# Two annealed layers of linear attention and gated MLP: evacuations and feature-map halves placed engine by engine, and a buffer of its own for the turned query weights

## The chip, the cores and the metric

The kernel runs on one core of one Trainium2 chip. The metric is device microseconds of that core, the median of several executions. Matmuls run on PE (TensorE), PSUM is emptied by ACT (ScalarE) or DVE (VectorE); POOL (GpSimd) does a share of one elementwise product; SP issues DMAs.

The profile's span (first to last instruction) is about 1.8 us shorter than the timed execution, so 391.3 us of span belong to 393.2 us of time.

## The reference, cut to what matters

```python
x = A_x                                     # 2048 tokens x 512, bf16
for layer in (0, 1):                        # both layers use the same weights
    x = x + A(layernorm(x))                 # attention with a linear kernel
    x = x + B(layernorm(x))                 # MLP with a rectified gate

# A: 32 heads of 16
q, k, v = split(x @ wqkv)
pq, pk  = q @ w_phi, k @ w_phi              # per head, 16 x 16
phi(p)  = concat(softmax(p), softmax(-p))   # 32 features per head
num, den = phi(pq) @ (phi(pk)^T @ v), phi(pq) @ sum(phi(pk))
A = (num / (den + 1e-6)) @ wo
# B
B = (relu(x @ W_gate) * (x @ W_up)) @ W_down   # 1376 hidden columns
```

## The kernel before

The kernel is a list of 2,096 small operations. Each has an engine, an assumed cost, its dependencies, the buffers that it takes, and a due time out of a table of numbers that was found offline by annealing (a random step-by-step search). A list scheduler in the kernel plays the operations through on the assumed costs, always taking the one that can start first and, among those, the one with the earliest due time. The order that comes out is the order in which instructions are written. Each engine then works through its own instructions strictly in that order.

The names that the argument needs: `Wk2` and `Wq2` are key and query weights multiplied ("folded") with `w_phi`. For this they are first turned (transposed): wk by matmuls, wq by DMA transposes. `ek` and `Eq` are exponentials of keys and queries, `phiK` the key features (`ek` times reciprocal sums `sk`), `vext` the values. "erq" matmuls (`q<-R,Eq`) give numerators and denominators of the attention; they are copied from PSUM to `N` and `DS`, and a chain of small DVE steps (`m`, `w`, `pr`, `o`) makes the output `o` of it. `oT` is `o` transposed, `xnTB` the transposed normalised input of the MLP, `gu` a gate and an up block, `hT` their product.

```python
def evac(eng, due, out_, in_, deps, takes, uses, name, cols=512):
    def copy():
        (nc.scalar.copy if eng == "ACT" else nc.vector.tensor_copy)(out=out_(), in_=in_())
    return op(eng, act(cols) if eng == "ACT" else dve(cols), due, copy, deps, takes, uses, name=name)
...
# turned weights: one buffer, inside a tile that the MLP uses later
wk, wT_ = (p_h.tiles[i][:, lo:lo + NB * D].rearrange("p (b f) -> p b f", b=NB)
               for i, lo in ((0, 512), (1, 0)))
p_wT = Pool([wT_])
...
# key features: whole tiles on one engine, one tile (BOTH) split
PHI = dict(POOL=[("POOL", 32)] * 2, DVE=[("DVE", 64)], BOTH=[("DVE", 32), ("POOL", 16), ("POOL", 16)])
...
# attention of a token tile, for each of three groups of erq matmuls: N and DS always on ACT
nc.scalar.copy(out=q[:, k, 0:3] if k < 2 else q[:, :, 3], in_=ps.t[...])
...
# MLP: relu(gate) and up both evacuated by ACT, product on DVE
a = op("ACT", act(cols), due_g(f0), relu, [g_], (), [gp, gu], name="rg")
u = op("ACT", act(cols), due_g(f0), copy, [u_, a], (), [up, gu], name="ru")
a = op("DVE", dve(cols, 2), due_g(f0), times, [a, u], (), [gu, h], name="hT", port=True)
...
q_fold = fold(A_wqkv[:, 0:D], Wq2, k_fold[-1], 5000, p["QF"] - 5000, ("ACT", "DVE"), True)
...
order = arrange(ops)
with tc.manual_schedule():
    free, filling = None, True
    for o in order:
        if o.eng == "PE":
            filling = filling and o.name != "kvz"
            if filling and free is not None:     # before the first key sums: fill planned gaps
                idle(max(0, int((o.start - free - 150) / FILL)))   # with matmuls on zeros
            free = o.start + o.spent
        o.emit()
```

The softmax here doesn't subtract the row's maximum and nothing guards it: scores larger than these inputs give would overflow.

## Time and profile before

| | before |
|---|---|
| time, median | 392.84 us (392.43 to 393.45, 3 runs) |
| span of the profiled run | 391.3 us |
| busy: PE, DVE, ACT, POOL | 383.4, 272.9, 256.1, 27.6 us |
| useful matmuls, back to back | about 373.3 us |
| holes and filler between matmul starts | 13.3 us |

First the head of the page of the kernel before: span, busy time by engine, and three rows of busy tenths in 40 slices of the span.

```profile
span 391.3 us, 7634 instructions
PE 383.4 (98%) x2836; PEld 232.7 (59%) x2836; DVE 272.9 (70%) x668; ACT 256.1 (65%) x683; POOL 27.6 (7%) x32
PE   8999998999999999999999999999999999999996
DVE  6998967889999778916863477689999624223422
ACT  5999999866857626852776379997863661641631
```

PE is busy throughout, but matmuls overlap in the pipe (a 128x512 matmul lasts 379 ns in the trace, and the next one starts after 216), so short holes hide in "busy". I therefore made a ledger from the starts of the matmuls in the trace. From each start to the next I take off what the first matmul is worth back to back, columns / 2.4 + 2.7 ns. The two constants are fitted to the trace: they give 216 ns for 512 columns, of which the trace has 4 in 0.86 us, and 56 ns for 128 columns, of which it has 32 in 1.79 us. What remains is a hole. Filler matmuls on zeros are worth nothing, so their whole time counts as a hole. Summed by stage, holes (13.3), the time before the first matmul (1.26), the worth of all useful matmuls (373.3) and the time from the last matmul's start to the end (3.42) make up the span.

Next, the windows of the kernel before: for each stretch its length, then busy us and number of instructions of PE, PEld (weight loads), DVE, ACT and POOL, the granted clock, the DMA share and GB/s.

```profile
57.00:71.00 14.00, 12.09 (x110) 7.64 (x109) 10.38 (x33) 13.52 (x45) 0.02 (x1) 1.00 0.01 2
71.00:110.00 39.00, 38.71 (x397) 29.35 (x395) 35.27 (x109) 27.97 (x87) 0.00 (x0) 1.00 0.36 61
250.00:258.00 8.00, 7.22 (x70) 4.76 (x68) 7.46 (x27) 8.00 (x28) 0.00 (x0) 1.00 0.10 19
258.00:300.00 42.00, 42.00 (x419) 31.22 (x417) 39.85 (x128) 30.57 (x99) 0.00 (x0) 1.00 0.34 66
```

The two lines in which PE falls behind its stretch are the changes from queries to attention, 57 to 71 in layer 0 and 250 to 258 in layer 1. There ACT is full (13.52 of 14, 8.00 of 8). The view of waits says for whom PE waited (us in total, times, longest):

```profile
PE q L560 <- DVE zero L537: 1.3, 1, 1.3
PE q L734 <- ACT N L741: 1.1, 2, 0.7
PE b L763 <- ACT oT L567: 0.9, 2, 0.6
PE b L643 <- DMA xnTA<-xn: 0.4, 1, 0.4
```

The start, by PE's timeline (start, length, line, output <- inputs, shape, count):

```profile
1.26 3.60 PE L560 MATMUL q<-zero 128*128 128x512 bf16 x8 [1.26 <-DVE zero L537]
4.65 1.53 PE L580 MATMUL b<-ident,hT 128*128 128x128 bf16 x12
8.61 1.46 PE L560 MATMUL q<-zero 128*128 128x512 bf16 x6
11.62 0.81 PE L560 MATMUL q<-zero 128*128 128x512 bf16 x3
21.08 1.89 PE L716 MATMUL b<-xnTA,Wq 128*128 128x512 bf16 x8
```

Eight warm-up matmuls at half rate (427 ns apart), then nine fillers (6 and 3) between real work, and the first query matmul at 21.1 us.

### The profile page before, as it was taken

The page shows a single profiled execution, that of the slowest core. Times are in us where ns is not written, and L with a number is a line of the kernel's source. Part 1 is how long each engine was busy: PE and PEld are TensorE (multiplying, and loading weights), DVE is VectorE, ACT ScalarE, POOL GpSimd, SP SyncE. Part 2 cuts the span into 40 slices and gives each one's busy share as a digit, 9 for nine tenths or more (in the row PEclk, how much of TensorE's full clock was granted, in tenths as well). Part 3 has the DMA queues.
Part 4 walks back from the last instruction along what each step waited for, and adds up shares of the span by engine and source line. Part 5 has one row for each costly group of instructions (what it writes and reads, how often), then busy time and mean ns, then how long its engine had stood idle before and what let it go on. Part 6 is the DMA issues. An engine that isn't in the chain of part 4 may idle for free.

```text
span 391.3 us, 7634 instructions
## 1 busy us (share of the span) xinstructions
PE 383.4 (98%) x2836; PEld 232.7 (59%) x2836; DVE 272.9 (70%) x668; ACT 256.1 (65%) x683; POOL 27.6 (7%) x32
## 2 busy tenths in 40 slices
PE   8999998999999999999999999999999999999996
PEld 5454554867755445544577655577765544445874
DVE  6998967889999778916863477689999624223422
ACT  5999999866857626852776379997863661641631
POOL 0264550000000000000000003000000000000000
PEclk9999999999999999999999999999999999999999
DMA  7668740123443213002110010022434302001010
GB/s 230 118 165 195 179 144 1 37 42 55 94 63 56 40 40 56 13 2 41 34 36 2 4 24 0 3 41 49 87 70 82 83 0 69 13 13 62 18 44 28
DMA packets 60870, 22.83 MB, mean 58 GB/s; under 512 B 52673, under 2 KB 59809, under 8 KB 60833
## 3 DMA queue, kind: packets, MB, share of 16 engines
q1 hardware_dynamic: 60416, 21.95, 26.0%
q8 instruction: 22, 0.36, 0.4%
q10 hardware_dynamic: 416, 0.39, 0.3%
q14 instruction: 16, 0.12, 0.1%
HBM read 7.91 MB, written 2.10 MB: 26 GB/s over the span
## 4 chain that ended last, share of the span: by engine, by line
PE 85%; ACT 8%; DVE 3%; DMA 2%; issue 1%; DVEq 0%
PE b L827 35%; PE b L861 19%; PE b L763 6%; PE b L643 6%; PE b L649 5%; PE b L716 4%; PE q L679 3%; PE b L803 3%; PE q L734 3%; ACT Eq L720 2%; ACT N L741 2%; ACT ek L646 2%; DMA xnTA<-xn 1%; PE q L560 1%; DMA oT<-o 1%
## 5 line engine op out<-in xcount | busy, mean ns | idle before, releaser
L827 PE MATMUL b<-xnTB,wgu 128*128 128x128 bf16 (+2 forms) x1200 | 149.2, 279 | 0.1
L827 PEld LDWEIGHTS <-wgu 128*128 128x128 bf16 x1200 | 97.6, 98 | 43.8 <-DVE X L767 0.2
L861 PE MATMUL b<-wd,hT 128*128 128x512 bf16 (+2 forms) x363 | 83.8, 373 | 0.0
L837 DVE TENSOR_TENSOR hT<-gu 128x512 bf16<-128x512 bf16 (+1 forms) x83 | 34.0, 411 | 62.6 <-ACT gu L834 62.5
L831 ACT ACTIVATE gu<-b 128x512 bf16<-128x512 f32 (+1 forms) x83 | 49.2, 605 | 32.4 <-PE b L827 31.7
L834 ACT CAST gu<-b 128x512 bf16<-128x512 f32 (+1 forms) x83 | 48.2, 583 | 28.6 <-PE b L827 27.7
L861 PEld LDWEIGHTS <-hT 128*128 128x128 bf16 (+1 forms) x363 | 34.8, 98 | 34.0 <-DVE hT L837 0.3
L741 ACT CAST N<-q 128x384 bf16<-128x384 f32 (+1 forms) x96 | 44.8, 540 | 3.7 <-DVE pr L756 1.5
L654 DVE TENSOR_REDUCE sk<-ek 128x64 f32<-128x1024 bf16 x32 | 38.4, 1212 | 8.2 <-ACT ek L646 8.1
L663 POOL TENSOR_TENSOR phiK<-ek,sk 128x512 bf16<-128x512 bf16 (+1 forms) x26 | 26.9, 1056 | 213.0 <-ACT sk L659 203.4
L720 ACT ACTIVATE Eq<-b 128x512 bf16<-128x512 f32 x64 | 39.2, 667 | 3.7 <-PE b L716 3.5
L646 ACT ACTIVATE ek<-b 128x512 bf16<-128x512 f32 x64 | 35.4, 612 | 3.7 <-PE b L643 3.4
L868 DVE SCALAR_TENSOR_TENSOR X<-b,rsB,X 128x512 bf16<-128x512 f32 (+1 forms) x33 | 23.5, 728 | 18.4 <-PE b L861 18.2
L763 PE MATMUL b<-wo,oT 128*128 128x512 bf16 x128 | 32.6, 379 | 1.1 <-ACT oT L567 0.9
L649 PE MATMUL b<-wv,xnTA 128*128 128x512 bf16 x128 | 32.5, 379 | 0.0
L643 PE MATMUL b<-Wk,xnTA 128*128 128x512 bf16 x128 | 32.1, 379 | 0.4 <-DMA xnTA<-xn 0.4
L716 PE MATMUL b<-xnTA,Wq 128*128 128x512 bf16 x128 | 31.5, 379 | 0.1
L741 ACT COPY DS<-q 128x48 f32<-128x48 f32 (+1 forms) x96 | 22.3, 284 | 10.2 <-PE q L734 8.6
L663 DVE TENSOR_TENSOR phiK<-ek,sk 128x1024 bf16<-128x1024 bf16 (+1 forms) x22 | 25.3, 1162 | 3.3 <-ACT sk L659 1.7
L734 PE MATMUL q<-R,Eq 128*128 128x144 bf16 x256 | 26.0, 226 | 1.2 <-ACT N L741 1.1
L734 PEld LDWEIGHTS <-Eq 128*128 128x128 bf16 x256 | 19.6, 98 | 10.4 <-issue 1.4
L767 DVE TENSOR_TENSOR X<-X,b 128x512 bf16<-128x512 bf16 x32 | 21.5, 673 | 1.9 <-PE b L763 1.7
(66 smaller groups left out, 373.0 us busy)
## 6 DMA issues: line engine op xcount, KB each, us to landing
out_dram<-X SPq DMA_DIRECT2D x15, 128.0 KB, 1.7
X<-in_A_x_dram SPq DMA_DIRECT2D x6, 256.0 KB, 3.7
wgu<-in_B_W_gate_dram SPq DMA_DIRECT2D x4, 344.0 KB, 3.4
wgu<-in_B_W_up_dram SPq DMA_DIRECT2D x4, 344.0 KB, 3.9
wd<-in_B_W_down_dram SPq DMA_DIRECT2D x5, 256.0 KB, 3.6
wv<-in_A_wqkv_dram SPq DMA_DIRECT2D x2, 256.0 KB, 4.3
wo<-in_A_wo_dram SPq DMA_DIRECT2D x4, 128.0 KB, 3.0
oT<-o SPq DMA_TRANSPOSE x28, 2.4
```

The lines of the kernel that those rows point to most:

```text
L643: k = op("PE", mm(4, 512), due, lambda: [nc.tensor.matmul(kp.t[:], lhsT=xnTA[c][:, b, cols], rhs=Wk2[:, b, :], start=(b == 0), stop=(b == ...
L649: v = op("PE", mm(4, 512), due_v, lambda: [nc.tensor.matmul(vp.t[:], lhsT=xnTA[c][:, b, cols], rhs=wv[:, b, :], start=(b == 0), stop=(b == ...
L663: e.tensor_tensor(out=ph.t[:].rearrange("p s (h f) -> p (s h) f", f=DH)[:, lo:lo + n], in0=ek.t[:].rearrange("p s (h f) -> p (s h) f", f=D ...
L716: q = op("PE", mm(4, 512), due(c, b), lambda b=b, qp=qp: [nc.tensor.matmul(qp.t[:], lhsT=Wq2[:, m, b * P:(b + 1) * P], rhs=xnTA[c][:, m, : ...
L720: done.append(op("ACT", act(512), due(c, b), lambda b=b, s=s, qp=qp: nc.scalar.activation(out=Eq[c][:, b, s, :], in_=qp.t[:], func=AF.Exp, ...
L734: pe.append(op("PE", mm(len(groups), GE), due, lambda ps=ps, groups=groups: [nc.tensor.matmul(ps.t[:, n * GE:(n + 1) * GE], lhsT=Eq[c][:, ...
L741: nc.scalar.copy(out=q[:, k, 0:3] if k < 2 else q[:, :, 3], in_=ps.t[:, 0:n * GE].rearrange("p (n c j) -> p n c j", n=n, j=HB)[:, :, lo:hi])
L763: a = op("PE", mm(4, 512), due + 3, lambda: [nc.tensor.matmul(yp.t[:], lhsT=oT.t[:, b, :], rhs=wo[:, b, :], start=(b == 0), stop=(b == NB ...
L827: nc.tensor.matmul(ps.t[:, q * W:(q + 1) * W], lhsT=wgu[:, s, b, g * P:(g + 1) * P], rhs=xT.t[:, b, 0:W], start=(b == 0), stop=(b == NB - 1))
L831: nc.scalar.activation(out=gu.t[:, 0, 0:cols], in_=gp.t[:, 0:cols], func=AF.Relu)
L834: nc.scalar.copy(out=gu.t[:, 1, 0:cols], in_=up.t[:, 0:cols])
L861: nc.tensor.matmul(yp.t[:, 0:c1 - c0], lhsT=h.t[:m, f * W + i * P:f * W + (i + 1) * P], rhs=wd[:m, f, c0:c1], start=(f == 0), stop=(f == N ...
```

## The change

The intent: let the same annealing that sets the due times also choose, one by one, whether an evacuation runs on ACT or DVE and whether a half of a key-feature tile runs on DVE or POOL. Both tables are new. The turned wq gets a second buffer, so that its DMA transposes need not wait for K's folds. Cut to its core:

```diff
+PLACE = (
+    "1101000000000000000010000000000000001100000010000000100000010000000000000000001010101000100000100001"
+    ...    # 397 places: 1 = the other engine
+PHI = dict(POOL=("POOL", "POOL"), DVE=("DVE", "DVE"), BOTH=("DVE", "POOL"))
 DUE = (
-    37902962, 37904246, ...
+    ...                                  # every due time is new
-    wk, wT_ = (... for i, lo in ((0, 512), (1, 0)))
-    p_wT = Pool([wT_])
+    wk, *wT_ = (... for i, lo in ((0, 512), (1, 0), (1, NB * D)))
+    p_wT = Pool(wT_)
     def evac(eng, due, ...):
+        both = {"ACT": ("ACT", act(cols), lambda: nc.scalar.copy(...), False),
+                "DVE": ("DVE", dve(cols), lambda: nc.vector.tensor_copy(...), False)}
+        ... return op(..., alt=both["DVE" if eng == "ACT" else "ACT"])
     # phi: two halves for every tile, each with ways for DVE and POOL
+            for k, e in enumerate(PHI[phi_eng]):
+                ways = {"DVE": ("DVE", dve(512), ...), "POOL": ("POOL", (1035, 1065), ...)}
     # N, DS and the up half of gu go through evac, so they may move too
-    q_fold = fold(A_wqkv[:, 0:D], Wq2, k_fold[-1], ...)
+    q_fold = fold(A_wqkv[:, 0:D], Wq2, None, ...)
+    for o, w in zip([o for o in ops if o.alt], PLACE):
+        if w == "1":
+            o.swap()
     order = arrange(ops)
```

By the order of instructions, 103 evacuations in balance move from ACT to DVE: 39 of 96 DS, 26 of 96 N, 28 of 83 up halves of gu, 7 vext, 3 xnTB. Of 64 phi halves POOL has 30, where it had the worth of 23. Useful matmuls are the same 2,819; filler falls from 17 to 11. The order changes on every engine.

## The prediction

> **What bounds it.** The matrix engine: PE is 98% busy on the page, granted clock 1.0. In the chain of waits four 128x512 matmuls take 0.86 us, 216 ns each. Scaled by columns (about 2.7 ns per instruction), the useful matmuls are worth about 373 of the 391.3 us (my estimate from those rates). The other 18: 1.3 before the first matmul, 3 after the last one starts, and 13.5 of holes and filler:
> - 0 to 20 us: 7.1. Eight warm-up matmuls start 427 ns apart instead of 216 (the Trainium skill, "TensorE: Matmul & The Clock Gate", Part 1, states a half-rate clock for the first ~3.4 us; the timeline agrees, 3.6 us) and sixteen weight-turning matmuls share it; nine more fillers and their gaps cost about 2.5.
> - 30 to 40: 0.5, behind a 4.6 us DMA transpose of xn; in the 80s 0.5.
> - 57 to 71 (layer 0, queries to attention): 3.4. ACT is busy 13.5 of 14 us, and the chain puts 38% of 60 to 72 on N evacuations and 24% on Eq exponentials, both ACT. Only here does an evacuation engine clearly hold PE.
> - Layer 1's transition, 250 to 258: 1.6, ACT 8.0 of 8.
> Elsewhere matmuls run back to back, so most moved work buys nothing.
>
> **What the change does.** Useful matmuls are identical; filler falls from 17 to 11. By the instruction order about 103 evacuations move from ACT to DVE (39 DS, 26 N, 28 gu, 7 vext, 3 xnTB, few others), and phi comes in halves: DVE 34 of 64 (was 41 halves' worth), POOL 30 (was 23). Costs in the trace: gu on ACT 592 ns, a 128x512 PSUM cast on DVE about 680; N on ACT 576/466; DS on ACT 288/275, on DVE about 200 (estimate); phi on DVE 1216 for both halves, 684 or more for one; on POOL 1116 per half. ACT falls from 256 to about 207 us, DVE rises from 273 to about 315, POOL from 27.6 to 34. The own buffer lets the four DMA transposes of wq start before 7.3 us, so Q enters the matrix stream earlier.
>
> **On the critical path.** Only the roughly 9 us of reducible holes count. Start: fewer fillers, earlier fold, -1.3. 57 to 71: DS, N and xnTB on the less busy DVE (10.4 of 14), -1.7. Layer 1's transition -0.7; others -0.5. New losses +0.5: DVE is already 9 to 10 of 10 us busy at 90 to 130 and 270 to 300 and gets more, with slower casts, and DVE and POOL can block each other ("SBUF — State Buffer", section "SBUF: two separate sides": an exclusive lock on the shared port pair; phi pieces on POOL spread from 0.61 to 2.1 us here, which fits).
>
> **Predicted: 389.0 us**, 8 in 10 within 386.6 to 391.8. Faster by over 2%: 0.04; within 2%: 0.94; slower by over 2%: 0.02.
>
> **What would show it.** PE still 98 to 99% busy, matmul means unchanged, 2830 matmuls; ACT clearly below full in 57 to 71; PE's waits for ACT (1.1 us for N, 0.9 for oT) roughly halved; DVE above 310; the first Q matmul well before 21.1 us.
>
> **What would make it wrong.** Filler hid real arrival times: if loads or fold evacuations land no earlier, holes replace filler and the start gains nothing. The attention's small DVE steps may queue behind casts, opening holes at 70 to 130 or 250 to 300. The other way: if start and both transitions close almost fully, 385 to 386.

## More of the kernel before

From 258 to 300 us PE has no gap although DVE is nearly full (39.85 of 42).

In the profiles of the first four experiments some 45 matmul records are missing, so all profiles were lined up with the program's own list of matmuls and a missing one counts as worked.

## The result, and the profile after

The ratio of two kernels is the mean time of the one's fast runs over that of the other's in the same rounds, so not quite the ratio of the medians quoted.

| | before | after |
|---|---|---|
| time, median of 6 | 393.02 us (392.43 to 393.56) | 392.23 us (391.51 to 392.95) |
| ratio to before | 1 | 0.9979 (0.9962 to 0.9995) |
| same, repeated on two other chips | 1 | 0.9987 (0.9963 to 1.0010), 0.9979 (0.9963 to 0.9994) |

The change gains about 0.2%, or 0.8 us, where 3.8 were predicted, and the time lies just outside the predicted range. The page of the changed kernel, the same rows:

```profile
span 390.9 us, 7625 instructions
PE 382.7 (98%) x2830; PEld 232.1 (59%) x2830; DVE 305.8 (78%) x783; ACT 223.0 (57%) x580; POOL 33.9 (9%) x36
PE   8999998999999999999999999999999999999996
DVE  6989979999998998649485797999999955333534
ACT  5999979746355535416726289985554350542311
```

DVE is busier by 33 us and ACT less by 33; PE's row is the same. The same windows of the changed kernel:

```profile
57.00:71.00 14.00, 12.95 (x139) 9.23 (x138) 11.52 (x45) 13.98 (x43) 0.00 (x0) 1.00 0.06 11
71.00:110.00 39.00, 38.73 (x365) 28.05 (x363) 38.10 (x120) 20.46 (x60) 1.19 (x1) 1.00 0.28 56
250.00:258.00 8.00, 7.54 (x95) 5.94 (x93) 7.41 (x28) 8.00 (x24) 0.00 (x0) 1.00 0.08 16
258.00:300.00 42.00, 41.66 (x392) 29.99 (x393) 41.82 (x142) 23.03 (x68) 0.00 (x0) 1.00 0.31 63
```

PE works 0.9 us more in 57 to 71 and 0.3 more in 250 to 258, as hoped. ACT, however, is still full in both, since other work came forward into the room. From 258 to 300 us PE has a gap that it did not have: DVE is now full to 41.82 of 42 while ACT is down to 23.03. The waits after:

```profile
PE q L590 <- DVE zero L567: 1.2, 1, 1.2
PE q L766 <- ACT DS L596: 0.5, 1, 0.5
PE b L634 <- DVE xn L816: 0.5, 1, 0.5
PE b L797 <- DMA oT<-o: 0.4, 1, 0.4
PE q L766 <- DVE DS L597: 0.4, 1, 0.4
PE q L766 <- DVE N L597: 0.3, 2, 0.2
```

The waits for ACT shrank, and waits for DVE (DS, N, xn) stand in their place. The start after:

```profile
1.19 3.60 PE L590 MATMUL q<-zero 128*128 128x512 bf16 x8 [1.19 <-DVE zero L567]
8.66 0.59 PE L590 MATMUL q<-zero 128*128 128x512 bf16 x2
10.54 0.40 PE L619 MATMUL b<-Wblk,hT 128*128 128x128 bf16 x4 [0.19 <-DMA hT<-in_A_wqkv_dram]
11.23 0.72 PE L634 MATMUL b<-ident,xn 128*128 128x128 bf16 x8 [0.29 <-DVE xn L654]
17.43 2.75 PE L748 MATMUL b<-xnTA,Wq 128*128 128x512 bf16 x12
```

Six fillers are gone and the first query matmul comes 3.6 us earlier, but real waits (for the DMA transposes of wq, for xn) appear where filler stood. The ledger of holes in us; the changed kernel was profiled three times. The line between 250 to 258 and 258 to 310 is drawn by time, and a hole near 258 falls to either side of it, so the two are summed as well:

| stage | before | after, three profiles | predicted change | measured change |
|---|---|---|---|---|
| before the first matmul | 1.26 | 1.19 | 0 | -0.1 |
| 0 to 20 | 7.14 | 6.60, 6.25, 6.43 | -1.3 | -0.5 to -0.9 |
| 20 to 57 | 0.65 | 0.52, 0.51, 0.31 | part of "others -0.5" | -0.1 to -0.3 |
| 57 to 71 | 3.36 | 1.92, 1.70, 1.92 | -1.7 | -1.4 to -1.7 |
| 71 to 250 | 0.47 | 1.17, 1.16, 1.18 | part of "new losses +0.5" | +0.7 |
| 250 to 258 | 1.61 | 0.95, 0.95, 0.95 | -0.7 | -0.7 |
| 258 to 310 | 0.16 | 1.51, 1.70, 1.12 | part of "new losses +0.5" | +1.0 to +1.5 |
| 250 to 310 together | 1.77 | 2.46, 2.65, 2.07 | | +0.3 to +0.9 |
| last matmul's start to the end | 3.42 | 3.81, 3.81, 3.79 | 0 | +0.4 |

One thing in the line 0 to 20 is not the change: matmuls at half rate count in part as holes, and the full clock comes at another time in each profile. By the trace's record of the granted clock it came at 6.84 us in the kernel before and at 6.40, 4.96 and 6.02 us in the three profiles of the changed kernel. At a like clock (7.14 us of holes with the full clock at 6.84 us before; after, 6.60 at 6.40 and, in c3, whose start is the same, 6.95 at 7.12) the start gained some 0.2 to 0.5 us.

For the profile on record the lines (without the sum line, and with -0.05 and -0.04 after 310 us) add up to 18.0 us before and 17.6 after, which is the difference of the spans, 0.4 us.

### The profile page after: what moved, and what is told of

It is laid out like the page before. It is cut to its first block, busy times and chain, and to the rows that moved or that the text cites. A ratio compares the mean times of both kernels' runs of the same rounds, so it can differ in the third digit from the quotient of the medians.

```text
span 390.9 us, 7625 instructions
## 1 busy us (share of the span) xinstructions
PE 382.7 (98%) x2830; PEld 232.1 (59%) x2830; DVE 305.8 (78%) x783; ACT 223.0 (57%) x580; POOL 33.9 (9%) x36
## 4 chain that ended last, share of the span: by engine, by line
PE 74%; DVE 13%; ACT 7%; DMA 2%; issue 2%; SPq 1%; DVEq 0%; ACTq 0%
PE b L861 29%; PE b L894 18%; PE b L674 6%; PE b L680 6%; PE b L797 4%; PE q L711 3%; PE b L748 3%; ACT Eq L752 3%; ACT N L596 2%; PE b L837 2%; DVE pr L790 1%; PE q L766 1%; DVE N L597 1%; DVE X L801 1%; DMA xnTA<-xn 1%
## 5 line engine op out<-in xcount | busy, mean ns | idle before, releaser
L694 POOL TENSOR_TENSOR phiK<-ek,sk 128x512 bf16<-128x512 bf16 x30 | 33.2, 1125 | 182.2 <-ACT sk L690 89.9
L596 ACT CAST gu<-b 128x512 bf16<-128x512 f32 (+1 forms) x55 | 32.3, 586 | 21.3 <-PE b L861 21.1
L752 ACT ACTIVATE Eq<-b 128x512 bf16<-128x512 f32 x64 | 38.2, 659 | 2.4 <-PE b L748 2.4
L596 ACT CAST N<-q 128x384 bf16<-128x384 f32 (+1 forms) x70 | 31.3, 487 | 8.3 <-PE q L766 4.3
L766 PE MATMUL q<-R,Eq 128*128 128x144 bf16 x256 | 27.8, 226 | 1.5 <-ACT DS L596 0.5
L649 ACT ACTIVATE lnA<-mvA,eps 128x1 f32<-128x1 f32 x32 | 9.1, 307 | 28.9 <-DVE mvA L644 28.5
L597 DVE CAST gu<-b 128x512 bf16<-128x512 f32 (+1 forms) x28 | 18.6, 663 | 8.6 <-PE b L861 8.3
L694 DVE TENSOR_TENSOR phiK<-ek,sk 128x512 bf16<-128x512 bf16 x34 | 23.3, 717 | 1.4 <-ACT sk L690 1.2
```

Of the source, the lines that this page charges most:

```text
L596: both = {"ACT": ("ACT", act(cols), lambda: nc.scalar.copy(out=out_(), in_=in_()), False), "DVE": ("DVE", dve(cols), lambda: nc.vector.ten ...
L694: e.tensor_tensor(out=ph.t[:].rearrange("p s (h f) -> p (s h) f", f=DH)[:, lo:lo + n], in0=ek.t[:].rearrange("p s (h f) -> p (s h) f", f=D ...
L752: done.append(op("ACT", act(512), due(c, b), lambda b=b, s=s, qp=qp: nc.scalar.activation(out=Eq[c][:, b, s, :], in_=qp.t[:], func=AF.Exp, ...
L766: pe.append(op("PE", mm(len(groups), GE), due, lambda ps=ps, groups=groups: [nc.tensor.matmul(ps.t[:, n * GE:(n + 1) * GE], lhsT=Eq[c][:, ...
```

## The experiments

All experiments keep an order that the scheduler made and alter it only when instructions are written: an operation is written for the other engine (`swap`), into another buffer, or at another place of the list; one leaves out the filler. No kernel is scheduled anew, so the useful matmuls of PE come in the order of the kernel that it is made from. All 15 were correct by the comparison with the reference, with one caveat told below:

| run | made from | ratio to before (95%) | median us |
|---|---|---|---|
| a1_after, c4_after | changed kernel, unaltered | 0.9987, 0.9979 | 392.39, 392.44 |
| a2_l1_back | changed | 1.0017 (0.9996 to 1.0039) | 393.75 |
| a3_all_back | changed | 1.0103 (1.0080 to 1.0127) | 396.91 |
| a4_before_buffer | before | 1.0000 (0.9978 to 1.0022) | 393.17 |
| b1_late_back | changed | 0.9976 (0.9962 to 0.9989) | 391.82 |
| b2_hr_later | b1 | 0.9975 (0.9960 to 0.9990) | 391.93 |
| b3_before_placed | before | 1.0431 (1.0416 to 1.0445) | 409.84 |
| b4_before_nofill | before | 1.0041 (1.0022 to 1.0060) | 394.22 |
| c1_one_buffer | changed | 1.0120 (1.0100 to 1.0140) | 398.14 |
| c2_phi_back | changed | 1.0046 (1.0030 to 1.0063) | 395.12 |
| c3_hoist | b1 | 0.9958 (0.9943 to 0.9974) | 391.66 |
| d1_one_buffer | changed | 0.9980 (0.9964 to 0.9997) | 392.74 |
| d2_hoist_both | c3 | 0.9949 (0.9932 to 0.9967) | 391.51 |
| d3_early_back | changed | 1.0017 (0.9996 to 1.0039) | 393.76 |

### The yardsticks

> The changed kernel again, unaltered, as the yardstick on this chip. Both theories: 0.998 of before, so about 0.8 us shorter. If it comes out at 1.000 or above, the difference on record is no more than the spread between chips.

> The changed kernel as the yardstick for the other three on this chip: 0.998 to 0.999 of before, its ledger of holes as in its first profile within 0.4 us in each stage.

0.9987 and 0.9979: the gain is small and repeats on other chips; in the first of the two the interval still includes none. Every stage of the ledger was within 0.4 us of the first profile.

### Layer 1's moved evacuations back to ACT

```diff
     order = arrange(ops)
+    for o in order[first_erq_of_layer_1:last_projection_of_layer_1]:
+        if o.alt and o.name in ("Q", "ru", "xnTB") and o.eng == "DVE":   # Q: N and DS, ru: up
+            o.swap()
```

> The changed kernel's order kept on every engine's list, but all evacuations of layer 1's attention stage that it moved to DVE (DS, N, up halves of gu, xnTB) go back to ACT. Saturation theory (the gain is given back because DVE is full there: 41.8 of 42 us busy from 258 to 300, ACT only 23): holes between matmuls from 258 to 310 shrink from 1.6 us to 0.6 or less, time 0.7 to 1.3 us below the changed kernel. Order theory (the new due times, not the placement, opened these holes): holes stay at 1.3 us or more, time within 0.3 us of the changed kernel.

Neither theory came out. The time rose to 1.0017. Holes from 258 to 310 were 1.26 us, no clear fall, but two holes of 0.34 and 0.33 us in the attention matmuls near 273 and 281 us were gone. From 250 to 258 us, however, they rose from 0.95 to 2.14. In the transition ACT is full, and there the placement is needed; after it, it hurts. One experiment had mixed two stages with opposite signs.

### All moved evacuations back, and the missing cell

```diff
+    for o, w in zip([o for o in ops if o.alt], PLACE):      # on the changed kernel's order
+        if w == "1" and o.name != "phi":
+            o.swap()
```

> The changed kernel's order, but every moved evacuation back on its former engine (phi halves stay as changed). Saturation theory: holes from 57 to 90 us rise from about 2.6 to 3.5 to 4.5 us, holes from 258 to 310 fall from 1.6 to 0.6 or less; the two nearly cancel and the time is within 0.7 us of the changed kernel. Order theory (order and placement were fitted together and only work together): slower than the changed kernel by 2 us or more, with holes in several stages.

1.0103, 4.5 us over the changed kernel's median: holes 16.9 us in all instead of 12.2, among them 2.65 from 57 to 71 (1.70 in the changed kernel on that chip), 1.41 from 110 to 250 (0.27) and 3.34 from 250 to 310 (2.65). PE's longest wait but the first tells where:

```profile
PE q L766 <- ACT DS L596: 3.2, 5, 1.0
```

The order theory is right: this order relies on its placement. From 71 to 110 us the holes come to 0.89 with and without the placement, against 0.39 before the change, but they are not the same holes. The changed kernel has three (0.32 us at 74, 0.19 at 81, 0.25 at 93 us); the first and the third wait for an N and a DS on DVE, and all three are gone here. In their place stands one of 0.69 us at 77 us that waits for an N on ACT. So this run does not tell order from placement there.

The other way round, the same moves at the order of the kernel before (phi left alone):

```diff
     order = arrange(ops)        # before's due times, before's engines
+    for o, w in zip(marks, PLACE):
+        if o is not None and w == "1":
+            o.emit = o.other     # the same evacuation on the other engine
```

> The kernel before with its own order and due times; the same evacuations are moved between ACT and DVE as in the change (phi stays as before). This is the missing cell of order by placement. Fit theory (each order needs the placement it was fitted with): 1% or more slower than before, 396 us or above, with holes where DVE gets casts in the attention stages. Independent theory (the placement is good in itself and the new order bad): 1% faster than before, about 389.

1.0431, with 30.1 us of holes in all instead of 13.3, of which 21.1 lie from 57 to 310 us (5.6 before). The four cells (phi goes with the order) are 392.7 us (old order, old places), 409.8 (old order, new places), 396.9 (new order, old places), 392.4 (both new): order and placement are one fit, and "the placement" has no worth of its own that could be added to the old order. A part of the 17 us may be owed to the method: the list positions were ACT's, and a DVE that meets them at other times makes later instructions of its list wait. Letting the scheduler make a new order with the old due times would have told the two apart, but it ran into a state in which no operation can go, so this was not measured.

### The late evacuations back to ACT

```diff
+    for o in order[worth(249.5):]:        # from 249.5 us of planned matmul work on
+        if o.alt and o.name in ("Q", "ru", "xnTB") and o.eng == "DVE":
+            o.swap()
```

> The changed kernel's order; evacuations that it put on DVE go back to ACT only from about 261 us on, after layer 1's transition, where ACT has room (23 of 42 us busy) and DVE has none. Late saturation theory: the two 0.33 us holes in the attention matmuls near 273 and 281 us vanish as they did in the run that put back the whole layer, the 0.95 us of holes at 250 to 258 stay, the 0.6 to 0.8 us hole near 306 behind a DMA transpose stays: time 0.4 to 0.8 us under the changed kernel. Rival (order and placement fit only together, wherever one is undone): new holes of 0.5 us or more open after 261 us, time equal to the changed kernel or above it.

As the late saturation theory had it. Holes from 258 to 310 fell from 1.51 to 0.60 us, those of 250 to 258 stayed at 0.95, and the time went to 391.82 us. The stretch in question, to be read against the same line of the changed kernel above:

```profile
258.00:300.00 42.00, 42.00 (x393) 30.08 (x391) 39.07 (x125) 27.79 (x90) 0.00 (x0) 1.00 0.35 67
```

DVE gets 2.75 us back, ACT takes 4.76, and PE is again without a gap. By ratio (0.9976 against 0.9979 to 0.9987 on other chips) the gain in time over the changed kernel is not resolved; by the holes it is 0.5 to 1.1 us, according to the profile of the changed kernel that it is set against. What is sure of it is 0.67 us: the holes near 273 and 281 us stand in all three profiles of the changed kernel (0.34 and 0.33 us) and in none of the runs with late evacuations put back (a2, b1, b2, c3, d2). Pieces of the chain that ended last in the changed kernel (start, length, what), at the second of these holes and at the one near 306 us:

```profile
279.79 0.59 DVE pr L790
280.38 0.14 DVE w L787
280.75 0.49 ACT N L596
281.28 0.28 PE q L766 x2
302.81 4.35 DMA oT<-o
307.21 0.82 PE b L797 x3
```

The first goes from DVE's small steps over an N on ACT to PE. The other stands behind a DMA transpose and is the subject of the next run.

### The transpose behind the late output transpose

```diff
+    hrT = order.pop(k)                    # DMA transpose of hr, four token tiles
+    order.insert(after_third_xnTB, hrT)
```

> The run above, and the four-tile DMA transpose of hr that was issued 1.6 us behind the late transpose of o at 302.8 us goes behind the next three transposes of xn on the queue. Queue theory (the big transpose delays the landing of the small one, 4.35 us instead of the median 2.4): the hole near 306 us falls from 0.6 to 0.8 us to 0.2 or less and the time by as much. DVE theory (o itself comes late from a full DVE): the transpose is issued earlier by a microsecond already in the run above, and moving the other one changes nothing.

The hole near 306 us is 0.60 in the changed kernel's profile, 0.45 in the run above and 0.15 here, but a hole of 0.38 us that b1's profile had not shown stands near 286 us, also before projections that wait for `oT`, and the time is the same. The waits for transposes of `o` vary from profile to profile (the one at 306 was 0.60, 0.83 and 0.25 in the three profiles of the changed kernel). This stays inconclusive.

### Filler

```diff
-        free, filling = None, True
+        free, filling = None, False
```

> The kernel before without the nine filler matmuls that follow the eight warm-up ones, nothing else changed. My prediction's theory (filler costs time of its own): holes and filler of the first 20 us fall from 7.1 to about 5.8, time 1.0 to 1.5 us less. Rival (filler stands only in waits for loads, statistics and evacuations): holes of the first 20 us stay within 0.3 us of 7.1 and the time within 0.5 us of before.

My theory is wrong. Without the nine fillers the holes of the first 20 us are 7.03 us instead of 7.14, and waits stand where the filler stood:

```profile
PE b L643 <- DVE Wk L567: 1.0, 1, 1.0
PE b L643 <- ACT xnTA L567: 0.7, 1, 0.7
```

In time the kernel even lost 0.4%, 1.5 us by the medians, which the rival (within 0.5 us) had not expected either. Its profiled run was its fastest (393.41 us; the others 393.85 to 396.08) and two of the others have a granted clock of 0.996, so a lower clock after the longer waits may be the reason; no such run was profiled, and it stays open.

### The own buffer

```diff
     order = arrange(ops)            # the kernel before, its order unchanged
+    wT_bufs[1].pool, wT_bufs[1].slot = Pool([wTq_]), 0   # turned wq elsewhere
```

> The kernel before with its own order, only the turned wq in a buffer of its own. Order theory of the start (the buffer pays only where the order lets folds and Q move forward): the four DMA transposes start at about 5.5 us instead of 7.3, but holes in the first 20 us stay at 7.1 plus or minus 0.3 and the time is within 0.3 us of before. Buffer theory: holes in the first 20 us fall by 0.5 us or more and the time falls by as much.

Ratio 1.0000, holes 6.82 instead of 7.14: nothing, as the order theory said (the full clock came at 4.14 us in this profile and at 6.84 in the one of the kernel before, so even the 0.3 us need not be the buffer's). Next the reverse, the changed kernel with one buffer:

```diff
+    wT_bufs[1].slot = wT_bufs[0].slot
```

> The changed kernel's order and placement, but wq is turned into the buffer that K's turned weights use, as before the change. Buffer theory (the order, which folds wq from 10 us on, needs the buffer): the four DMA transposes cannot start before about 7.4 us instead of 5.5, folds of wq wait for them, holes of the first 20 us rise from 6.3 to 6.6 to 7.5 or more and the time by 0.9 us or more. Rival (buffer worth nothing here, loads of x set the start): holes stay under 6.9 and the time within 0.4 us of the changed kernel.

Slower by 1.2%, with 12.5 us of holes at the start, but not for the reason meant. The list holds one DMA transpose of wq ahead of K's evacuation into the same quarter of the buffer, so K's evacuation waited for a DMA:

```profile
6.47 0.39 PE L620 MATMUL b<-Wblk,hT 128*128 128x128 bf16 x4
10.70 1.46 PE L620 MATMUL b<-Wblk,hT 128*128 128x128 bf16 x12 [3.83 <-DVE hT L597]
11.95 1.91 PE L681 MATMUL b<-wv,xnTA 128*128 128x512 bf16 x4
```

After the 3.83 us of idle time the matmuls ran at half rate once more, four of 512 columns in 1.9 us instead of 1.03, until about 16.4 us. By the order of the list a quarter of the folded wq was also made of K's data in this run, and the comparison did not notice. The run shows what a wrong order in a shared buffer costs and what a hole of that length costs on top; of the buffer's worth it says nothing. The mended run writes the four transposes behind K's last fold:

> The one-buffer run, mended: in the first try the list kept one DMA transpose of wq ahead of one of K's evacuations, so K's fold waited 3.8 us for a DMA that in the kernel before comes after it, and a part of wq was folded from K's data. Here the four transposes stand behind K's last fold. Buffer theory: first transpose at about 7.4 us instead of 5.5, folds of wq wait, holes of the first 20 us rise from 6.3 to 6.6 to 7.5 to 9, time 1 to 2.5 us over the changed kernel. Rival (buffer worth nothing, x sets the start): holes under 6.9, time within 0.4 us.

The transposes start at 6.96 us instead of 5.47, and the folds of wq wait:

```profile
7.22 1.03 PE L681 MATMUL b<-wv,xnTA 128*128 128x512 bf16 x4
8.51 1.03 PE L675 MATMUL b<-Wk,xnTA 128*128 128x512 bf16 x4
10.81 0.40 PE L620 MATMUL b<-Wblk,hT 128*128 128x128 bf16 x4 [1.27 <-DMA hT<-in_A_wqkv_dram]
11.80 0.40 PE L620 MATMUL b<-Wblk,hT 128*128 128x128 bf16 x4 [0.60 <-DMA hT<-in_A_wqkv_dram]
```

But V and K start at 7.22 and 8.51 us, 0.6 earlier than in the changed kernel (7.80 and 9.10), and the first query matmul only 0.6 later (18.05 against 17.43). The earlier V and K are not the buffer's doing: in this profile the full clock came at 4.29 us (6.40 in the changed kernel's), so the turned weights were ready sooner (ACT's first copy of them starts at 5.09 instead of 5.67 us). Holes of the first 20 us are 7.22 us against 6.25 to 6.60, between the two theories and in a profile that fell on the slowest of its runs; the time is 0.3 us over the changed kernel's on the same chip, as the rival said, and the ratio, 0.9980, is the same (0.9979). By the holes of this one profile the buffer is worth 0.6 to 1.0 us, by the time nothing that can be seen; which is right stays open. It is the new order that brings most of the queries' advance (18.05 us without the buffer, 21.08 in the kernel before), and the buffer is a condition for writing the transposes so early.

### Phi

```diff
+    for o, w in zip([o for o in ops if o.alt], PLACE):
+        if w == "1" and o.name == "phi":
+            o.swap()
```

> The changed kernel with all phi halves back on the engine they had before; all else as changed. Off-path theory: matmuls are dense wherever phi is placed, so holes change by less than 0.5 us in each stage and the time by less than 0.6 us. Rival (phi on GpSimd relieves the full DVE while layer 1's keys are made, so it carries part of the gain): holes from 71 to 250 us rise by 0.8 us or more.

My off-path theory is wrong: 395.12 against 392.44 us on the same chip. Holes from 110 to 250 us rise from 0.3 to 2.2, in three holes of 0.6 us before the key sums:

```profile
185.04 0.58 PE L711 MATMUL q<-vext,phiK 128*128 128x129 bf16 x7 [0.40 <-DVE phiK L694]
186.93 0.62 PE L711 MATMUL q<-vext,phiK 128*128 128x129 bf16 x8 [0.43 <-ACT vext L596]
```

The kernel before had all of layer 1's phi on DVE or nearly so and only 0.08 us of holes there. The third hole, at 200.5 us, waits for a `vext` on DVE, and the `vext` on ACT above is late because its engine stood 1.89 us for a small DVE step of the layernorm (`mvA`). So all three come from DVE: with casts added to it, some of phi has to leave it, and one part of the placement pays for another.

### Layer 0's transition

```diff
+    for o in order[worth(47.0):worth(62.5)]:
+        if o.alt and o.name in ("Q", "ru", "xnTB", "oT") and o.eng == "DVE":
+            o.swap()
```

> The changed kernel's order; only the moved evacuations of layer 0's transition (about 57 to 71 us: DS, N, xnTB, oT) go back to ACT. Placement theory (this is the term of 1.7 us in my prediction): holes from 57 to 71 us rise from 1.9 to 3.2 to 3.8, as before the change, time 1.2 to 1.9 us over the changed kernel. Rival (the new order alone shortened this stage): holes stay under 2.4, time within 0.5 us.

Between the two theories and nearer the first: holes from 57 to 71 us rise from 1.92 to 2.86, against 3.36 before the change. The window of this run:

```profile
57.00:71.00 14.00, 12.02 (x125) 8.38 (x123) 10.83 (x37) 14.00 (x47) 0.00 (x0) 1.00 0.06 11
```

The placement makes about 0.9 of the 1.4 us that this stage gained, and the new order the other 0.5. The median is 1.3 us above the changed kernel's on the same chip.

### A better version

Two small moves on DVE's list, on top of the late put-back. Near 257 us the aggregation and centring for the next MLP tile stood behind a DS evacuation that itself waited 0.56 us (by the trace for an N on ACT):

```diff
+    for k in (agg, x):                 # aggr and xn of the second tile of layer 1's transition
+        order.insert(stat, order.pop(k))   # right behind the statistics
```

> A try for a better version: the late put-back, and in layer 1's transition the aggregation and centring for the second tile are taken ahead of the DS evacuation that they stood behind on DVE. Queue-order theory: the 0.62 us hole before the transpose of xn near 257 us falls to 0.2 or less, holes of 250 to 258 from 0.95 to about 0.45, time 0.9 to 1.3 us under the changed kernel (0.9 from the late put-back). Rival: the hole only moves to the next attention matmul, which waits for that DS, and nothing is gained.

The 0.62 us hole at 257 went, and one of 0.56 us came at 259, before the matmuls that wait for the evacuation of that transpose: the rival was half right, and the time, 391.66 us, is 0.8 us under the changed kernel's on that chip instead of 0.9 to 1.3. So that evacuation went up too:

```diff
+    order.insert(at, order.pop(e))     # evacuation of xnTB ahead of the later small attention steps
```

> The hoist run, and the evacuation of that tile's transpose goes up DVE's list too, since the hole had moved from 257 to 259 us in front of the matmuls that wait for it. Queue-order theory: holes from 250 to 310 fall from 1.6 us to 1.2 or less; time 1.0 us or more under the changed kernel (392.4), about 391.2. Rival: the next wait is as long again, holes stay at 1.5 or more.

Holes from 250 to 310 us are 1.26 us, against 2.07 to 2.65 in the changed kernel, nearer the first theory, and the time is 391.51 us, 0.9949 of before (0.9932 to 0.9967) and 0.9 us under the changed kernel. On that chip the changed kernel stands at 0.9979, so of the version's 0.5% some 0.3 come from undoing late moves and two positions in one list. It is the fastest version and still within 2% of all others but b3.

## Why the prediction was wrong

I predicted 389.0 us in a range of 386.6 to 391.8 and got 392.2. That it would be within 2% was right, and so was the frame: PE-bound, about 13.5 us of holes, nothing to gain outside them. The terms:

- *"57 to 71: ... -1.7"*. Right in size (-1.4 to -1.7), and by d3 two thirds of it is due to the placement. My sign for it ("ACT clearly below full") was wrong: ACT is at 13.98 of 14, because freed time was filled with work brought forward (17 N evacuations there instead of 15, and two of gu, for 6 DS less).
- *"Layer 1's transition -0.7"*. Right for 250 to 258 us (-0.7).
- *"New losses +0.5"*. This is the step that failed; the term measured +2.1 to +2.6 us. It is 0.7 from 71 to 250, 1.0 to 1.5 from 258 to 310, and 0.4 at the end. The mechanism was named ("DVE is already 9 to 10 of 10 us busy ... and gets more"), but I took it for a small remainder, although the numbers of the kernel before were there: the windows above give DVE 3.7 us left of 39 from 71 to 110 and 2.2 of 42 from 258 to 300, and after the change its busy time is 2.8 and 2.0 us higher there. Of 258 to 310, 0.67 us is shown to be the placement (two holes that go whenever it is undone there), the rest is mostly the hole before projections that wait for `oT`, 0.25 to 0.83 us by the profile, whose cause stays open. From 71 to 110 two of the three new holes wait for an N and a DS on DVE, but putting them back opens another (a3), so order and placement are not told apart. The 0.4 us at the end, present in every kernel with the new order and its phi (3.77 to 3.82 us; 3.57 with phi put back), are no loss of the engines: from the last matmul's start to the landing of the last output it is 2.52 us before and 2.50 after, and the difference comes behind that landing (0.90 and 1.31 us). Why is not known.
- *"Start: fewer fillers, earlier fold, -1.3"*. Too large: -0.5 to -0.9, and some 0.2 to 0.5 at a like clock. Filler is not a cost where it stands in a wait (b4), which I had written down as a possible error and not used. The buffer as such gives nothing in the old order (a4); in the new one it stays open between nothing and about 1.0 us (d1).
- *"Others -0.5"*: -0.1 to -0.3.
- *"Elsewhere matmuls run back to back, so most moved work buys nothing"*. True of the old order, wrong of the new one: undoing phi alone costs 2.7 us, undoing the evacuations 4.5, and using the new places in the old order 17. A dense stage is dense because of its schedule. The new order is dense only with these moves.
- DVE rose to 305.8 us, not 315, and ACT fell to 223.0, not 207. I priced each moved evacuation at the mean duration of its group, and that was a third too much, because instructions of one engine overlap in the trace. The durations of all ACT instructions sum to 332.6 us before and 276.6 after, 56.0 less, but the busy time, in which an overlap counts once, falls by 33.1. A DS of 48 columns that starts while its predecessor on ACT still runs ends about 0.10 us after it, though its own mean duration is 0.288; an N of 384 columns ends 0.38 us after it, with a mean of 0.576. On DVE the same steps are about 0.115 and 0.47 us, so that moving these two makes neither shorter.

So the gain expected in the transitions was made, and most of it was given back elsewhere. The lines for 0 to 71 us and 250 to 258 gained 2.8 us, the rest lost 2.4. Whether the annealing's cost model did not see the late losses or saw them and found them free was not tested.

## What to carry to other kernels

When one engine is 98% busy, make a ledger of its holes by stage before and after; a change that moves a hundred instructions can have a net effect smaller than its largest entries (here -1.4 and +1.4 us in two stages, and -0.4 in all). Here moving work to a second engine paid in the stages where the first was full and the second was not, and undoing it paid late in layer 1, where the second was full. Price a moved instruction by what it adds to its engine's busy time, not by its mean duration. Do not credit or blame a placement without the order it was fitted with, and when undoing one in an experiment, look at the list of instructions for what now stands in front of what.

## What the Trainium skill lacked or had wrong

- "TensorE: Matmul & The Clock Gate", Part 1: a half-rate clock for the first ~3.4 us, said to vary by run. Here the half rate lasted from the first matmul at 1.26 us to 6.83 us in the kernel before (128-column matmuls 107 ns apart until then, 56 after), so 5.6 us; by the trace's record of the granted clock it was 2.9 (a4) to 5.9 us (c3) over the 17 profiles. After the 3.83 us hole of the one-buffer run it lasted from 10.70 to 16.43 us, 5.7 us. That an idle window of this length cools the clock agrees with the page's table.
- No page that I read says that the profile's row of granted clock does not show the first cold stretch: it stands at 1.00 for the window 0 to 13 us, in which matmuls of 512 columns start 427 ns apart; the trace's record of the clock begins only at 6.84 us.
- "VectorE: DVE Perf Modes", section on the TRN2 errata, table of cycles from PSUM to SBUF: not wrong here. By estimates worked out from its cycles and clocks, 512 columns take 570 ns on ScalarE and 658 on VectorE; the trace has 592 and 599 for casts of gu on ACT and 682 on DVE. DS with 48 columns on ACT is estimated at 183 ns and N with 384 at 463; those of the kernel before that start after their predecessor has ended take 198 (10 of them) and 478 (8). The means of all, 288 and 576, are longer because most start while the predecessor still runs. On DVE 198 and 545 stand against 175 and 525.
- "SBUF — State Buffer", section "SBUF: two separate sides", gives an exclusive lock between DVE and GpSimd. My prediction took the spread of phi on POOL, 0.61 to 2.1 us, as agreeing with it (a clause that is cut): the 0.61 us belongs to quarter tiles. Of the 20 halves before, 17 lie between 1052 and 1057 ns and one takes 2102; after the change they are 1052 to 1563 ns with a median of 1057. No run here isolates the lock.
- "Perfetto Trace Analysis" does not say that a profile can lack some matmul records: 44 of 2,830 in the first profile of the yardstick.
